# Decode kernel, two passes of attention and feed-forward: new constants in its planner, a new order of loads, two instead of four K units kept

## The chip, the cores and the metric

One core of a Trainium2 chip runs the whole program. The time is device microseconds of one execution; a kernel's figure is the median of its runs, and runs of two kernels are compared only when they were taken in turn on the same chip. "The span" is the profiled execution from its first to its last record, about 1.8 us shorter than the time of that run. PE is the engine that multiplies matrices (PEld its weight loads), DVE the vector engine, ACT the scalar engine, SPq the queue that issues the loads, SBUF the core's memory on the chip.

## The reference, cut to what matters

An attention block with cached K and V and a gated feed-forward block, applied twice, for a batch of four and one token each. Weights and caches are the same in both passes, so every K and V byte is needed twice.

```python
B, Sq, D = 4, 1, 512
Hq, Hkv, Sk, Dh = 32, 8, 8192, 128          # k_cache, v_cache: (B, Hkv, Sk, Dh) bf16
...
x = x + attention(layernorm(x), k_cache, v_cache, wq, wo)
x = x + (silu(xn @ w_gate) * (xn @ w_up)) @ w_down       # xn = layernorm(x)
x = x + attention(layernorm(x), k_cache, v_cache, wq, wo)
x = x + (silu(xn @ w_gate) * (xn @ w_up)) @ w_down
```

K is 64 MiB and so is V; read in both passes this is 256 MiB. SBUF holds all weights and 11 slots of 1 MiB, so nearly everything must stream in twice.

## The kernel before

A **unit** is 1 MiB of K or V: half of one head's cache for one batch. The program is made by a small planner: steps with guessed durations for PE, DVE and ACT, and a list of loads in a fixed order. The planner plays them through, and the order in which it starts them is the order of the instructions in the program. What the chip then does waits only on semaphores. The order of the loads is a string of tokens: `K` the next K unit, `P` the next two K units in one load of 2 MiB, `a`/`b` a V unit of the first or second pass (batch, head, half), `A`/`B` both halves in one load, `c` a second-pass V unit that needs no load because its first-pass copy is **kept** in its slot, `wq wo0 wg1 ...` weight pieces. The code is cut, and its comments are added here.

```python
class Plan:
    HOP = 0.06
    PAGE = 5.0          # us to fetch 256 PE instructions
    PAGE_N = 256
    LOAD_LEAD = 2.1     # us from issue to first data
    LOAD_TAIL = 2.1     # us from last data to landing
    ...
                s.start = t                       # a slot is free, the queue issues
                sp_at = t + 0.35
                dma_at = max(dma_at, t + self.LOAD_LEAD) + s.us
                s.end = dma_at + self.LOAD_TAIL
    ...
ORDER = ("c100 c101 P c260 x P c300 c301 c261 wq P wg1 c120 P c340 P K K c341 P P wo1 A06 P wo0 P a010 K c240 "
    ...
NSLOT = 11
KM = (4, 0, 0, 0)       # K units of batch 0..3 that stay in their slots for the second pass
    ...
        if u not in kept_k:
            st.slot_of = home[u]      # the slot comes free after these matmuls
    ...
        if u[1] == 1 and ("k", 0) + u[2:] in kept_k:
            home[u] = ("k", 0) + u[2:]            # second pass of a kept unit: no load
        else:
            loads[u] = load_pair(u)
```

A kept unit saves one load and holds one of the 11 slots for as long as it waits. In each batch a serial chain lies between the passes: output projection, feed-forward, the next query projection. Until it is done the batch's second-pass K can be loaded but not consumed.

## Time and profile before

| what | before |
|---|---|
| time, median of 4 | 638.88 us (638.27 to 640.04) |
| span of the profiled run | 636.9 us |
| bytes read from memory | 256.12 MB, 402 GB/s over the span |
| PE / DVE busy | 397.1 / 402.7 us |
| load queue busy, as a share of 16 DMA engines | 97.7% |
| landing of the last load, and the end after it | 626.25 us, 10.7 us |

The queue of loads is the bound; PE and DVE have over a third of the span to spare. A list made from the trace is used all through this text: for each load its issue, its landing (the completion semaphore's last update), the distance from the landing before, and how far **ahead** it was issued, meaning the time from its issue to the landing of the load before it. A load that is ahead enough lands one transfer time after the previous one; a load that is not leaves a gap.

### The profile page before, as it was taken

To read this page: it belongs to the slowest core of one execution; us is meant where nothing else is said; L and a number is where in the kernel's file an instruction comes from. 1 tells how busy PE (TensorE), PEld (TensorE's weight loads), DVE (VectorE), ACT (ScalarE), POOL (GpSimd) and SP (SyncE) were. 2 spreads that over 40 slices of the span, in tenths; PEclk is the share of its full clock that TensorE was granted. 3 is DMA by queue.
4 is the path that set the end of the run, shared out by engine and by line. 5 is a ranking of instruction groups with operands and counts; after the bars stand their busy time and mean duration, and the time that the engine had idled before them with its cause. 6 is when DMAs were issued, how large, how long until landed. Compare 5 with 4: busy or idle time off the path is not lost.

```text
span 636.9 us, 18609 instructions
## 1 busy us (share of the span) xinstructions
PE 397.1 (62%) x8689; PEld 205.1 (32%) x8689; DVE 402.7 (63%) x615; ACT 40.4 (6%) x107; POOL 1.8 (0%) x8
## 2 busy tenths in 40 slices
PE   0375444454786675677576665578667676856686
PEld 0221211113542141135421241333431244721265
DVE  4477764365236958876579777366667863489832
ACT  1000200002000020000200100000100020000100
POOL 1000000000000000000000000000000000000000
PEclk9997686657557767667667778555575667568686
DMA  8999999999989999999999999999999999999991
GB/s 356 423 426 412 405 417 423 420 418 401 387 348 400 422 418 419 420 412 421 402 408 419 422 425 428 417 408 420 418 408 421 415 419 421 417 409 419 423 425 65
DMA packets 37237, 257.32 MB, mean 404 GB/s; under 512 B 3492, under 2 KB 9384, under 8 KB 10664
## 3 DMA queue, kind: packets, MB, share of 16 engines
q1 hardware_dynamic: 37160, 256.14, 97.7%
q8 instruction: 68, 1.11, 0.7%
q14 instruction: 9, 0.07, 0.0%
HBM read 256.12 MB, written 0.00 MB: 402 GB/s over the span
## 4 chain that ended last, share of the span: by engine, by line
DMA 63%; PE 18%; DVE 16%; issue 2%; SPq 0%; ACT 0%
DMA pool<-in_A_k_cache_dram 39%; DMA pool<-in_A_v_cache_dram 18%; DVE pool L606 12%; PE ps L622 7%; PE ps L763 5%; DMA wq_sb<-in_A_wq_dram 3%; PE ps L472 2%; DMA wo_sb<-in_A_wo_dram 2%; DMA wq_sb<-in_A_k_cache_dram 2%; DVE wq_sb L606 1%; PE ps L809 1%; PE ps L726 1%; DVE ps L790 1%; PE ps L681 1%; PE ps L873 1%
## 5 line engine op out<-in xcount | busy, mean ns | idle before, releaser
L606 DVE STREAM_TRANSPOSE pool<-pool 128x2048 uint32<-128x2048 uint32 x116 | 264.8, 2300 | 70.8 <-DMA pool<-in_A_k_cache_dram 70.6
L622 PE MATMUL ps<-pool,qpad 32*32 32x512 bf16 x3840 | 190.6, 543 | 127.2 <-DVE pool L606 120.7
L622 PEld LDWEIGHTS ps<-pool,qpad 32*32 32x32 bf16 x3840 | 54.6, 108 | 240.1 <-DVE pool L606 179.6
L763 PE MATMUL ps<-pool,pp 128*32 128x256 bf16 x1936 | 100.0, 366 | 43.1 <-DMA pool<-in_A_v_cache_dram 31.6
L763 PEld LDWEIGHTS ps<-pool,pp 128*32 128x32 bf16 x1936 | 57.5, 122 | 81.6 <-DMA pool<-in_A_v_cache_dram 42.8
L790 DVE STREAM_TRANSPOSE ps<-ps 128x256 f32<-128x256 f32 x62 | 28.4, 458 | 74.7 <-PE ps L763 74.4
L645 ACT ACTIVATE pp<-ps,negm 128x512 bf16<-128x512 f32 x32 | 21.6, 686 | 329.6 <-DVE negm L641 306.5
L726 PE MATMUL ps<-oT,wo_sb 128*128 128x4 bf16 x640 | 23.0, 167 | 12.6 <-DVE oT L794 9.2
L726 PEld LDWEIGHTS ps<-oT,wo_sb 128*128 128x128 bf16 x640 | 20.7, 103 | 24.7 <-DVE oT L794 16.7
L641 DVE TENSOR_REDUCE negm<-ps 128x1 f32<-128x512 f32 x32 | 19.9, 683 | 12.1 <-PE ps L622 12.1
L472 PE MATMUL ps<-xnT,wq_sb 128*128 128x4 bf16 x640 | 18.3, 166 | 12.1 <-DMA wq_sb<-in_A_wq_dram 11.4
L472 PEld LDWEIGHTS ps<-xnT,wq_sb 128*128 128x128 bf16 x640 | 17.7, 104 | 14.5 <-DMA wq_sb<-in_A_wq_dram 11.5
L606 DVE STREAM_TRANSPOSE wq_sb<-wq_sb 128x2048 uint32<-128x2048 uint32 x8 | 18.1, 2290 | 3.5 <-DMA wq_sb<-in_A_k_cache_dram 3.4
L681 PE MATMUL ps<-ident,pp 128*128 128x128 bf16 x128 | 16.0, 311 | 6.3 <-DVE pp L670 5.8
L622 PE MATMUL ps<-wq_sb,qpad 32*32 32x512 bf16 x256 | 13.2, 547 | 8.5 <-DVE wq_sb L606 8.5
L458 ACT ACTIVATE lnv<-var,eps_sb 128x4 f32<-128x4 f32 x10 | 3.0, 298 | 218.0 <-DVE var L453 218.0
L681 PEld LDWEIGHTS ps<-ident,pp 128*128 128x128 bf16 x128 | 12.7, 143 | 12.5 <-DVE pp L670 7.6
L792 DVE TENSOR_REDUCE osum<-ps 128x4 f32<-128x32 f32 x62 | 11.9, 191 | 2.1
L794 DVE TENSOR_TENSOR oT<-osum,invL 128x4 bf16<-128x4 f32 x62 | 10.5, 169 | 2.1
L670 DVE TENSOR_SCALAR pp<-pp,alpha 128x512 bf16<-128x512 bf16 x32 | 9.0, 346 | 1.8 <-ACT alpha L663 1.8
L690 ACT ACTIVATE pp<-ps 128x1024 bf16<-128x1024 bf16 x8 | 8.2, 1024 | 26.9 <-PE ps L681 26.9
L438 PE MATMUL ps<-xx,onesm 128*128 128x32 f32 x20 | 6.3, 410 | 5.3 <-DVE xx L433 4.3
(68 smaller groups left out, 149.4 us busy)
## 6 DMA issues: line engine op xcount, KB each, us to landing
pool<-in_A_k_cache_dram SPq DMA_DIRECT2D x86, 1024.0 KB, 9.7
pool<-in_A_v_cache_dram SPq DMA_DIRECT2D x82, 1024.0 KB, 10.0
pool<-in_A_k_cache_dram SPq DMA_DIRECT2D x15, 2048.0 KB, 15.8
pool<-in_A_v_cache_dram SPq DMA_DIRECT2D x10, 2048.0 KB, 16.6
wq_sb<-in_A_k_cache_dram SPq DMA_DIRECT2D x6, 1024.0 KB, 13.6
wq_sb<-in_A_wq_dram SPq DMA_DIRECT2D x1, 4096.0 KB, 22.0
wo_sb<-in_A_wo_dram SPq DMA_DIRECT2D x4, 1024.0 KB, 16.2
wq_sb<-in_A_k_cache_dram SPq DMA_DIRECT2D x1, 2048.0 KB, 10.3
```

What stands on the lines that cost most here:

```text
L472: op("pe", lambda e: e.matmul(ps[:, bk * BW + h * B:bk * BW + (h + 1) * B], lhsT=wq_sb[:, kt, h * Dh:(h + 1) * Dh], rhs=xnT[:, kt * B:(kt ...
L606: op("dve", lambda e: e.transpose(v, v), reads=keys, writes=keys)
L622: op("pe", lambda e: e.matmul(ps[32 * c:32 * (c + 1), a * BW:(a + 1) * BW], lhsT=qpad[rows, qbuf, es_, g, :], rhs=ap[h][rows, :, es_ // 2, ...
L641: op("dve", lambda e: e.tensor_reduce(negm[:, q, a:a + 1], bank(a), AX.X, ALU.max, negate=True), reads=[f"pb{a}"], writes=[f"negm{q}_{a}"])
L645: op("act", lambda e: e.activation(pblk(q)[:, :, a, :], bank(a).rearrange("p (t j) -> p t j", j=32), ACTF.Exp, bias=negm[:, q, a:a + 1], s ...
L670: op("dve", lambda e: e.tensor_scalar(seg, seg, alpha[:, q, a:a + 1], None, op0=ALU.mult), reads=[f"pp{q}_{a}", f"alpha{q}"], writes=[f"pp ...
L681: op("pe", lambda e: e.matmul(stg[:, t * P:(t + 1) * P], lhsT=pp[:, q, blk * P:(blk + 1) * P], rhs=ident[:], is_transpose=True, start=True ...
L726: op("pe", lambda e: e.matmul(ps[:, OPJ * BW + nq * B:OPJ * BW + (nq + 1) * B], lhsT=wo_sb[:, h, nq * P:(nq + 1) * P], rhs=oT[:, l, h, :], ...
L763: op("pe", lambda e: e.matmul(ps[32 * n:32 * (n + 1), bk * BW:bk * BW + 256], lhsT=pp[:, q, col:col + 32], rhs=v[:, 8 * f:8 * (f + 1), 32 ...
L790: op("dve", lambda e: e.transpose(blk, blk), reads=[f"pb{bk}"], writes=[f"pb{bk}"])
L792: op("dve", lambda e: e.tensor_reduce(osum[:], diag, AX.X, ALU.add), reads=[f"pb{bk}"], writes=["osum"])
L794: op("dve", lambda e: e.tensor_tensor(oT[:, l, g * REP:(g + 1) * REP, b], got, invL[:, q, g * REP:(g + 1) * REP], ALU.mult), reads=[f"pb{b ...
```

## The change

The intent: make the planner's picture of loads and of instruction fetch closer to the chip, and search an order that does well on average when landings come late. The new model charges a load 1.05 us or more when the queue has less than 2.0 us of data left at its issue, and a charge that fades from 1.05 us to nothing where the queue has 2.0 to 3.7 us left. By the planner's own tail of 2.1 us, that is 5.8 us ahead of a landing. The order that came out of the search gives up two kept K units.

```diff
-    PAGE = 5.0
+    PAGE = 5.8
+    PAGE_IDLE = 3.8
-    LOAD_LEAD = 2.1
+    LOAD_LEAD = 2.0
+    LOAD_SOFT = 1.05
+    LOAD_EASE = 3.7
+    def late(self, ahead):
+        if ahead < self.LOAD_LEAD:
+            return max(self.LOAD_LEAD - ahead, self.LOAD_SOFT)
+        return max(0.0, self.LOAD_SOFT * (self.LOAD_EASE - ahead) / (self.LOAD_EASE - self.LOAD_LEAD))
-                dma_at = max(dma_at, t + self.LOAD_LEAD) + s.us
+                dma_at += self.late(dma_at - t) + s.us
+                page = self.PAGE if there < dma_at else self.PAGE_IDLE
-ORDER = ("c100 c101 P c260 x P c300 c301 c261 wq P wg1 c120 P c340 P K K c341 P P wo1 A06 P wo0 ...
+ORDER = ("P P c120 c241 P wd1 c370 x wq c121 wo2 P P K K c371 P P P a021 P a060 a040 c240 P a061 ...
-KM = (4, 0, 0, 0)
+KM = (2, 0, 0, 0)
-            return PL.load(4.914, fn, u0, u1)      # a pair
+            return PL.load(4.924, fn, u0, u1)
-                return PL.load(2.505, fn, u)       # one unit
+                return PL.load(2.51, fn, u)
... (the rest of ORDER is cut)
```

No operation on the chip is added or removed except the two loads and their two transposes (and that 22 instead of 27 loads are pairs).

## The prediction

> **What bounds the kernel now.** I read the page first (time slices, queues, chain), then a table of stretches around the only visible dip, then what the queue that issues the loads waited for there, and last each load in the trace from issue to landing (its completion semaphore).
>
> ```profile
> DMA  8999999999989999999999999999999999999991
> GB/s 356 423 426 412 405 417 423 420 418 401 387 348 400 422 418 419 420 412 421 402 408 419 422 425 428 417 408 420 418 408 421 415 419 421 417 409 419 423 425 65
> ...
> q1 hardware_dynamic: 37160, 256.14, 97.7%
> q8 instruction: 68, 1.11, 0.7%
> ...
> DMA 63%; PE 18%; DVE 16%; issue 2%; SPq 0%; ACT 0%
> ```
>
> The reader is to see that one load queue keeps the 16 DMA engines busy for 97.7% of the span and that the rate is flat at 410 to 428 GB/s in nearly every slice. PE and DVE are busy 62% and 63% and are not the bound; their shares of the chain are short waits between loads. So the end is set by: start, plus bytes over rate, plus stretches in which the queue ran dry, plus the work after the last landing. The slices have one real dip, at about 175 to 191 us, so I cut the stretch finer:
>
> ```profile
> 180.00:184.00 4.00, 3.00 (x125) 2.71 (x123) 0.69 (x3) 0.00 (x0) 0.00 (x0) 0.50 1.00 416
> 184.00:194.00 10.00, 9.02 (x240) 4.39 (x236) 3.36 (x5) 0.00 (x0) 0.00 (x0) 0.66 0.78 274
> 194.00:204.00 10.00, 4.82 (x100) 1.66 (x88) 7.45 (x6) 0.00 (x0) 0.00 (x0) 0.68 1.01 421
> 204.00:610.00 406.00, 273.80 (x5682) 135.25 (x5683) 283.74 (x421) 28.19 (x75) 0.00 (x0) 0.65 1.01 418
> ```
>
> The last two columns are the DMA share and GB/s. From 204 to 610 us the queue is never short (418 GB/s on average, shares at 1.01). From 184 to 194 it is. The waits of the issuing queue and its issues say why:
>
> ```profile
> SPq L92 <- PE ps L622: 12.4, 3, 10.1
> SPq L62 <- PE ps L763: 10.2, 4, 8.8
> ...
> 175.70 0.33 SPq L92 DMA_DIRECT2D pool<-in_A_k_cache_dram  x1
> 176.69 10.76 SPq L92 DMA_DIRECT2D pool<-in_A_v_cache_dram  x2
> 188.13 18.36 SPq L92 DMA_DIRECT2D pool<-in_A_k_cache_dram  x11
> ```
>
> Between about 177 and 187 us no load can be issued: all 11 slots hold a unit (a unit is 1 MiB of K or V), and PE works through the feed-forward and query chain of batch 0 before it can consume second-layer K. The load issued at 187.12 lands 5.75 us after the one before it, where 2.48 us is usual. **That is 3.3 us lost, and it is the only load of 216 that came too late.** For the rest, the distance between landings is 2.48 us for 1 MiB alone and 4.89 us for 2 MiB in one transfer, plus some 12 us spread thinly over the kernel (0.1 us every fifth load, 0.5 to 1.2 us at ten or so places). These fall on loads issued 5 to 13 us ahead too, so an order of loads does not cure them. The last landing is at 626.25; 10.7 us of serial work (output projection, last feed-forward, store) follow.
>
> **What the Trainium skill says.** "Perfetto Trace Analysis", section "Identifying the Most-Contended Engine", wants DMA judged by memory rate, not by busy engines; here both agree. "DMA: Bandwidth & Descriptors", section "Where 436 GB/s comes from", puts the fabric ceiling at 435 GB/s; the flat 418 to 428 is 96 to 98% of it, so no schedule can make the bytes much faster. The same page, section "Measured", gives 1 MB 341 GB/s and 16 MB 425: the trace agrees with the trend only weakly, 1 MiB per 2.48 us being 423 GB/s and 2 MiB per 4.89 us 429, because queued loads overlap. "Runtime: NRT & Kernel Launch", section "Instruction fetch mechanics", has the instructions refilled in 16 KiB blocks of 256 and the cost mostly hidden. The trace agrees on the size (68 packets, 1.11 MB); hidden it is not on PE (weight loads of the score matmuls wait 53.5 us for "issue"), but it hardly shows on the load queue.
>
> **The change part by part.** All of it is the plan: the constants of the scheduler's model, the order of loads, and how many K units of batch 0 stay in SBUF for the second layer (KM from 4 to 2). No operation differs.
>
> 1. *Bytes.* I counted the tokens of both orders. Before: 16 K pairs and 96 single K tokens, 4 of these kept, so 124 K units loaded; 107 V units; 231 MiB. After: 14 pairs and 100 singles, 2 kept, so 126 K; V again 107 (21 kept in both): 233 MiB. Two more units of 2.48 us: **+4.96 us**, on the path, since the queue is the bound.
> 2. *Pairs.* Before 16 K, 7 + 4 V = 27 two-MiB transfers; after 14 + 4 + 4 = 22. A pair saves 2 x 2.48 - 4.89 = 0.07 us; five fewer: **+0.35 us**.
> 3. *Weights.* The same ten pieces and the query weights, earlier or later: 0.
> 4. *DVE and PE.* Two K units more to transpose at 2.30 us each: 4.6 us of DVE, which is 63% busy: hidden. Matmul counts are equal.
> 5. *The stall at the first chain.* The question is whether the new order removes the 3.3 us. I wrote both orders as lists of loads with running sums (2.48, 4.89, and 2.25 to 2.96 us for weight pieces). Before, the last weight that batch 0's chain needs is at 164.0 of this sum; after it, 164.2. Slots held through the chain: before, 4 K + 2 V of batch 0 and 1 V of batch 1; after, 2 K + 4 V. The slots are full at 176.4 before and 176.6 after. The built instruction order of PE is the same there too: down-projection, two V units, query projection, one K unit, two V units, more K. So the two units given back on the K side are taken again on the V side, and **the dry spell should come again**. One gain: the gate weights are there at 159.3 and the output weights at 152.1 (before, 156.5 for the last of these), so the chain may start about 1 us sooner. I take 0.5 us off.
> 6. *The other three chains.* Between the last first-layer V of a batch and the first K of its second layer the sums leave 35, 35 and 17 us of loads in the new order, as in the old, where none of the three ran dry: 0. The beginning has the query weights third pair later (sum 27.2 instead of 19.7), with 11 slots, two weight pieces and the query weights queued, which reach to about 47 us by the landing times, while K is consumed from about 36.5: no dry spell. I allow +0.3 us for something small.
>
> Sum: 638.8 + 4.96 + 0.35 - 0.5 + 0.3 = 643.9. An author picks an order because it does well, and the model's new curves may see a stall that I cannot see by counting, so I lean a little lower: **643.4 us**.
>
> **The rivals.** (a) *The new order removes the dry spell*: 638.8 + 5.3 - 3.3 = 640.8. For it: the order was chosen over delayed landings, and this dip is what such a choice would go for. Against: the slot count above. (b) *The change wins*, below 638: it would need more than 5.3 us back, and the trace has only 3.3 us of late loads and a fixed 10.7 us tail; only if the thin 12 us were due to the order. I see no sign. (c) *PE or a new dry spell becomes the limit*: rotating units through 11 slots with only two kept K to free at once after the chain, or the long runs of K (13 in a row in PE's order), could starve the queue again: 3 to 5 us more, 646 to 649. For it: kept V are held longer than kept K. Against: in such runs before, loads were issued 5 us or more ahead throughout.
>
> **Range and chances.** Low end: rival (a) with run-to-run scatter (the three runs span 638.27 to 640.04), 640.2. High end: the stall stays and another of its size comes, 647.0. Two per cent is 12.8 us: faster needs more than every idle microsecond of the queue, 0.01; slower needs three stalls on top of the bytes, 0.02; within, 0.97.
>
> **What would show each step.** Bytes read from memory should rise from 256.1 to 258.2 MB. Landings should stay 2.48 and 4.89 us apart; if they don't, the rate is not fixed and my sum falls. The last landing should move from 626.25 to about 631, with 10.7 us after it; a changed tail is a step that I left out. The slice at about 185 us should dip again: if it is flat, rival (a) holds and step 5 was wrong; a dip elsewhere is rival (c). If the total falls although the bytes rose, the thin losses were the schedule's after all, and that would make the prediction wrong.

## The result, and the profile after

| what | before | after |
|---|---|---|
| time, median of 4 | 638.88 us | 643.79 us (642.20 to 644.54) |
| ratio, 95% interval | | 1.0071 (1.0047 to 1.0096) |
| span of the profiled run | 636.9 us | 640.4 us (the fastest of its four) |
| last landing, and the end after it | 626.25, 10.7 us | 629.71, 10.7 us |
| PE / DVE busy | 397.1 / 402.7 us | 396.0 / 407.5 us |

The kernel became 0.7% slower, by some 4.9 us; that counts as the same at a threshold of 2%, but it is clear of the noise.

The page of the kernel after, its slices of DMA, its load queue and its memory line:

```profile
DMA  8999999999999999999999999999999999999992
GB/s 362 396 425 419 425 415 412 417 426 389 404 359 423 422 418 421 420 418 421 417 418 422 419 421 424 427 419 397 397 422 421 420 417 422 382 410 421 423 425 86
...
q1 hardware_dynamic: 38168, 258.23, 98.0%
...
HBM read 258.22 MB, written 0.00 MB: 403 GB/s over the span
```

The reader is to see the same picture with 2.1 MB more in it: the same flat rate and the same dip in the twelfth slice (359 now, 348 before). The load queue is no less full than it was, and it has more to carry. The same stretches as those of before in the prediction (the last two columns are the DMA share and GB/s):

```profile
180.00:184.00 4.00, 3.09 (x116) 2.83 (x112) 0.70 (x4) 0.00 (x0) 0.00 (x0) 0.50 1.01 420
184.00:194.00 10.00, 7.32 (x192) 3.44 (x192) 7.60 (x8) 0.00 (x0) 0.00 (x0) 0.79 0.84 325
194.00:204.00 10.00, 5.19 (x120) 1.71 (x128) 8.17 (x5) 0.00 (x0) 0.00 (x0) 0.73 1.01 426
204.00:614.00 410.00, 272.11 (x5712) 131.37 (x5696) 283.26 (x423) 28.18 (x75) 0.00 (x0) 0.65 1.01 417
```

The dry spell at 187 us is still there, milder in this run: 325 GB/s in place of 274. The issuing queue's waits from 170 to 195 us say that it is the same wait, for matmuls that free a slot:

```profile
SPq L62 <- PE ps L772: 11.7, 4, 8.6
SPq L92 <- PE ps L631: 9.7, 2, 9.2
SPq L62 <- PE ps L631: 3.1, 1, 3.1
```

What was bought with the two units is seen in the list of issues: the last column is the median time from issue to landing. First the kernel before, then the kernel after:

```profile
pool<-in_A_k_cache_dram SPq DMA_DIRECT2D x86, 1024.0 KB, 9.7
pool<-in_A_v_cache_dram SPq DMA_DIRECT2D x82, 1024.0 KB, 10.0
```

```profile
pool<-in_A_k_cache_dram SPq DMA_DIRECT2D x92, 1024.0 KB, 11.6
pool<-in_A_v_cache_dram SPq DMA_DIRECT2D x88, 1024.0 KB, 12.0
```

Loads wait about 2 us longer in a deeper queue, and there are more of them. Before, 38 loads of one unit were issued 5.5 to 6 us ahead; after, none was. But those 38 landed 2.48 us (median) after the load before them, as loads issued 10 us and more ahead do (2.49). **The depth was paid for with two loads and bought nothing that the chip had been charging.**

The landings of the two profiled runs, summed up, with 2.48 us a unit, 4.89 a pair and the weights' own times taken as the base:

| term | before to after |
|---|---|
| first landing (9.15, then 8.72) | -0.4 us |
| two more units | +5.0 us |
| five fewer pairs | +0.35 us |
| the late load at 187 us (3.3, then 1.0) | -2.3 us |
| thin losses spread over the kernel (11.7, then 12.6) | +0.9 us |
| last landing (626.25, then 629.71) | +3.5 us |

Most of the thin losses have one shape: a single landing about 1 us late, every 65 to 85 us. In the changed kernel these are seven of 1.0 to 1.24 us, 7.8 of its 12.6 us, all on loads issued 6 to 16.5 us ahead. Their cause is open (see the last section).

### The profile page after: what moved, and what is told of

Same layout as the page of the kernel before. It is cut to its first block, busy times and chain, and to the rows that moved or that the text cites. A ratio compares the mean times of both kernels' runs of the same rounds, so it can differ in the third digit from the quotient of the medians.

```text
span 640.4 us, 18628 instructions
## 1 busy us (share of the span) xinstructions
PE 396.0 (62%) x8689; PEld 202.1 (32%) x8689; DVE 407.5 (64%) x617; ACT 40.4 (6%) x107; POOL 1.8 (0%) x8
## 3 DMA queue, kind: packets, MB, share of 16 engines
HBM read 258.22 MB, written 0.00 MB: 403 GB/s over the span
## 4 chain that ended last, share of the span: by engine, by line
DMA 67%; PE 16%; DVE 13%; SPq 3%; issue 1%
DMA pool<-in_A_k_cache_dram 39%; DMA pool<-in_A_v_cache_dram 19%; DVE pool L615 10%; PE ps L631 7%; PE ps L772 4%; DMA wq_sb<-in_A_k_cache_dram 4%; DMA wq_sb<-in_A_wq_dram 3%; SPq L92 3%; DMA wo_sb<-in_A_wo_dram 2%; PE ps L481 1%; DVE wq_sb L615 1%; PE ps L818 1%; PE ps L882 1%; PE ps L690 1%; PE ps L735 1%
## 5 line engine op out<-in xcount | busy, mean ns | idle before, releaser
L615 DVE STREAM_TRANSPOSE pool<-pool 128x2048 uint32<-128x2048 uint32 x118 | 269.8, 2301 | 64.7 <-DMA pool<-in_A_k_cache_dram 64.2
L772 PEld LDWEIGHTS ps<-pool,pp 128*32 128x32 bf16 x1936 | 55.9, 120 | 88.0 <-DMA pool<-in_A_v_cache_dram 46.9
L481 PEld LDWEIGHTS ps<-xnT,wq_sb 128*128 128x128 bf16 x640 | 17.6, 103 | 11.4 <-DMA wq_sb<-in_A_wq_dram 7.1
L690 PE MATMUL ps<-ident,pp 128*128 128x128 bf16 x128 | 14.3, 283 | 2.4 <-DVE oT L803 1.4
L690 PEld LDWEIGHTS ps<-ident,pp 128*128 128x128 bf16 x128 | 11.2, 131 | 8.8 <-DVE selw L710 4.0
L818 PE MATMUL ps<-xnT,wu_sb 128*128 128x4 bf16 x280 | 8.9, 167 | 0.9 <-DVE hT L874 0.5
```

What stands on the lines that cost most here:

```text
L481: op("pe", lambda e: e.matmul(ps[:, bk * BW + h * B:bk * BW + (h + 1) * B], lhsT=wq_sb[:, kt, h * Dh:(h + 1) * Dh], rhs=xnT[:, kt * B:(kt ...
L615: op("dve", lambda e: e.transpose(v, v), reads=keys, writes=keys)
L690: op("pe", lambda e: e.matmul(stg[:, t * P:(t + 1) * P], lhsT=pp[:, q, blk * P:(blk + 1) * P], rhs=ident[:], is_transpose=True, start=True ...
L772: op("pe", lambda e: e.matmul(ps[32 * n:32 * (n + 1), bk * BW:bk * BW + 256], lhsT=pp[:, q, col:col + 32], rhs=v[:, 8 * f:8 * (f + 1), 32 ...
L818: op("pe", lambda e: e.matmul(ps[:, bk * BW + (fo - f0) * B:bk * BW + (fo - f0 + 1) * B], lhsT=w_sb[:, kt, fo * P:(fo + 1) * P], rhs=xnT[: ...
```

## The experiments

The theory, called **counting** below: the time is the loads, one after the other at a fixed distance, plus what is lost where a load is issued too late, about 4 us or less ahead. (The first expectation still said about 2 us; the limit was moved before the ten-slot runs.) The first rival is **depth**, the changed kernel's own model: loads issued up to 5.8 us ahead lose time, so a deeper queue is worth bytes. The second is that the new constants change the program through the placement of instructions on PE and DVE. All experiments computed the right result.

### Bytes without the new order: two K units kept, old order, old constants

```diff
-KM = (4, 0, 0, 0)
+KM = (2, 0, 0, 0)      # in the kernel before
```

> The old order and the old constants with two instead of four K units of batch 0 kept: two units more to load, no other edit. Counting theory (the time is the loads at 2.48 us a unit, plus the loads issued too late, about 2 us or less before the one ahead has landed): plus 4.96 us, minus the 3.3 us of the dry spell at 187 us if the two freed slots end it, so 640.5 us; 643.8 if the spell stays or a new one comes elsewhere (a late load after 350 us is possible, where two K pairs and two V pairs follow each other). Rival (the order itself, not the bytes, made the change slower): about 638.9, as before.

Measured: 643.19 us (before in these rounds 638.53), ratio 1.0073 (1.0055 to 1.0090). This one line costs what the whole change costs. The two freed slots did end the spell at 187 us, but another came at 370 us: a load issued 1.27 us ahead, 2.7 us lost. Its stretches:

```profile
184.00:194.00 10.00, 5.12 (x144) 2.65 (x144) 6.19 (x6) 0.00 (x0) 0.00 (x0) 0.76 1.01 416
...
368.00:378.00 10.00, 7.22 (x162) 6.27 (x162) 5.01 (x18) 1.12 (x2) 0.00 (x0) 0.75 0.80 307
```

From 184 to 194 the rate is 416 GB/s now, and the share is whole; the hole has moved. So 4.96 less 3.3 plus 2.7 is 4.4, and 4.7 was measured. The rival "the order, not the bytes" falls. The new order with the same two kept units, run in the same rounds (the next experiment), took 643.72: the order by itself adds or saves nothing clear of the noise.

### The constants alone, in both directions

The order and number of kept units of one kernel with the planner constants of the other.

```diff
# e2: the kernel after
-ORDER, KM of after
+ORDER, KM of before
# e3: the kernel before
-ORDER, KM of before
+ORDER, KM of after
```

> Old order and old number of kept units with the new constants of the scheduler's model: the same loads in the same order; only where PE and DVE instructions stand can move. Counting theory: as before, 638.9, within 1 us, the one late load at 187 us included. Rival (the new constants alone change the time through the order on PE): outside 637.5 to 640.5.

> New order and two kept K units with the old constants of the model: what the order and the kept units do without the new constants. Counting theory: as the changed kernel, 643.8 within 1 us, one late load at about 187 us of 1 to 3 us. Rival (the constants made the difference): near 639.

Measured: 638.89 us for the old order under the new constants, ratio to before 1.0003 (0.9986 to 1.0020); 643.72 us for the new order under the old constants, ratio 1.0074 (1.0053 to 1.0095). So the constants act through the order that they choose; whatever else they do is within the noise (0.2%, some 1.3 us). The late load is in both traces: 3.5 us lost at 187 us in the first, 2.6 us in the second (issued 1.36 us ahead, where the profiled run of the changed kernel had 1.94). The stretch of the spell, in the first and in the second:

```profile
184.00:194.00 10.00, 7.96 (x240) 3.90 (x240) 3.36 (x5) 0.00 (x0) 0.00 (x0) 0.83 0.81 302
```

```profile
184.00:194.00 10.00, 7.72 (x198) 3.50 (x192) 6.19 (x8) 0.00 (x0) 0.00 (x0) 0.75 0.78 302
```

Both ran at 302 GB/s there. So the changed kernel's milder spell was probably that run's more than the order's: it was also the fastest of its four, by 1.2 us. That is one trace of each, so it is not shown.

### What a pair is worth

```diff
-"... P c260 x P ... A06 ..."     # in the kernel before, all 27 pairs
+"... K K c260 x K K ... a060 a061 ..."
```

> The kernel before with each of its 27 two-MiB loads split in two loads of 1 MiB at the same place: a pair is worth 2 x 2.48 - 4.89 = 0.07 us by the landings, so counting theory expects 27 x 0.07 = plus 1.9 us, 640.8. Rival (pairs are worth nothing at this queue depth): 638.9. Rival (pairs save an issue and a late load each): over 643.

Measured: 639.88 us, ratio 1.0016 (0.9998 to 1.0035). The 27 pairs together are worth 1.0 to 1.35 us by ratio and by medians, 0.04 to 0.05 us each, a little less than the 0.07 of the landings; the interval's low end, 0.9998, does not exclude no effect at all.

### How far ahead must a load be issued: ten slots

Both kernels were run with one slot less, so that the same loads are issued later.

```diff
-NSLOT = 11
+NSLOT = 10
```

> The changed kernel with 10 instead of 11 slots: the same loads, each issued later, since a slot comes free later. Counting theory (a load costs extra only when it is issued under about 4 us before the landing ahead of it, and then only what is missing): three dry spells before 200 us (loads 18, 44 and 59 issued 0 to 9 us after the one ahead has landed), a few of 1 us later, some 663 us in all. Rival, depth theory (the new constants: any load issued under 5.8 us before the landing ahead loses up to 1 us): about 677 us.

> The kernel before with 10 instead of 11 slots. Here some forty loads will be issued 3 to 4 us before the landing ahead of them, which is what tells the two theories apart: the spacing of their landings is 2.48 us if depth is worth nothing down to there, or up to 3.5 us if it is. Counting theory: about 688 us in all. Rival, depth theory (soft loss below 5.8 us): about 708 us.

Measured, in one execution each, so that their state is unknown: 664.52 us for the changed kernel and 685.68 for the kernel before (before with 11 slots beside them: 637.66). Counting had said 663 and 688, depth 677 and 708 (both from the planner's arithmetic, with the old and the new constants). The changed kernel's trace has its three spells before 210 us, of 1.1, 11.4 and 5.3 us. The second trace holds loads at all distances, so the curve that the change is about can be read from it directly. The distance between landings of 1 MiB loads, by how far ahead they were issued:

| ahead, us | loads | median distance, us |
|---|---|---|
| 3 to 3.5 | 20 | 3.27 |
| 3.5 to 4 | 14 | 3.25 |
| 4 to 4.5 | 11 | 2.83 |
| 4.5 to 5 | 17 | 2.49 |
| 5 to 5.5 | 12 | 2.47 |
| 5.5 to 6 | 14 | 2.47 |
| 10 and more | 35 | 2.48 |

So this run lost about 0.8 us at 3 to 4 us ahead, and nothing in the medians from 4.5 on. On the point that was to tell the theories apart, the expectation for counting (2.48 us at 3 to 4 ahead) was wrong; it did not fit the theory's own limit of about 4 us either, and the 688 came from a planner that charges a load under 4.2 us ahead.

The loss at 3 to 4 us is of this run, and not shown as a rule of the distance alone: its single loads there took from 2.43 to 4.60 us, and the ten loads of 1 MiB that were issued 3 to 4 us ahead in the ten other traces took 2.46 to 3.11 (median 2.5). That nothing is lost from 4.5 us on, by the medians, is in these traces too: 17 loads at 4.5 to 5, 69 at 5 to 5.5 and 200 at 5.5 to 6, each group with a median of 2.48. The new constants let a loss run on to 5.8, and there the kernel before had most of its shallow loads. Two equal stretches in the middle, first of this ten-slot run, then of the kernel before, show the same in the rate:

```profile
380.00:450.00 70.00, 43.68 (x843) 20.17 (x834) 42.18 (x62) 4.10 (x10) 0.00 (x0) 0.60 0.98 394
450.00:520.00 70.00, 46.87 (x950) 24.16 (x942) 40.96 (x75) 5.25 (x15) 0.00 (x0) 0.52 0.97 371
```

```profile
360.00:430.00 70.00, 44.01 (x956) 23.77 (x952) 43.28 (x71) 4.61 (x12) 0.00 (x0) 0.70 1.01 420
430.00:500.00 70.00, 49.41 (x996) 23.52 (x988) 47.93 (x76) 4.75 (x13) 0.00 (x0) 0.56 1.01 416
```

With ten slots the queue really is too short (394 and 371 GB/s); with eleven it is not (420 and 416, as 417 in the long stretch of the changed kernel).

The planner itself, played without a chip, shows how the curve chose. These are its own guesses, no measurements: with the new constants it ends before's order at 640.5 us and the new one at 637.9; with `LOAD_SOFT` set to 0 at 632.1 and 636.5. The chip's spans are 636.9 and 640.4. It is the soft term alone that turned the two orders round in the model; without it the difference is 4.4 us, and the chip's is 3.5 in the spans and 4.9 in the medians.

### One more slot for one more load

```diff
-KM = (2, 0, 0, 0)      # in the kernel after
+KM = (1, 0, 0, 0)
```

> The changed kernel with one K unit of batch 0 kept instead of two: one more unit to load, one more free slot while batch 0's chain runs. Counting theory: plus 2.48 us for the unit, minus the late load at 187 us (1.0 to 2.6 us in the two runs of this order so far), so plus 0 to 1.5 us over the changed kernel: 643.8 to 645.3 us, and no landing gap at 187 us. Rival (the late load does not come from held slots): 646.3 us with the gap still there.

Measured: 644.77 us, ratio to before 1.0108 (1.0093 to 1.0123), so 6.9 us above before's 637.85 in its own rounds. The changed kernel was 4.9 us above before in its rounds. One kept unit less therefore costs 1.0 us by the bare times, which are of different rounds, and 2.0 to 2.4 us by the differences and the ratios; only the first lies in the expected 0 to 1.5. What the trace settles is the spell. Its stretch is full in this kernel:

```profile
184.00:194.00 10.00, 7.98 (x187) 3.41 (x184) 7.50 (x9) 0.00 (x0) 0.00 (x0) 0.67 1.01 411
```

The load that was late is now issued 4.2 us ahead and loses 0.2 us. So held slots do make the spell, and a unit (2.48 us) is a poor price for 1 to 2.6 us of spell.

### A version that should beat both

A search over orders with the soft loss cut to what the ten-slot trace shows gave two candidates.

```diff
-    LOAD_LEAD = 2.0 / LOAD_SOFT = 1.05 / LOAD_EASE = 3.7 / PAGE = 5.8 / PAGE_IDLE = 3.8
+    LOAD_LEAD = 1.9 / LOAD_SOFT = 0.8 / LOAD_EASE = 2.7 / PAGE = 5.2 / PAGE_IDLE = 4.2
-KM = (2, 0, 0, 0)
+KM = (3, 0, 0, 0)      # f1, with a new ORDER of 43 pairs; f2 has (4, 0, 0, 0) and 30 pairs
```

> An order found by search with the scheduler's late-load curve cut to what the ten-slot runs show (no loss from about 4.7 us before the landing ahead): 232 units (three K and 21 V kept), 43 pairs, no late load at batch 0's chain. Counting theory against before: plus 2.48 us for one unit, minus 16 more pairs at 0.05 to 0.07 us = 0.8 to 1.1, minus 3.3 us of dry spell: about 637.0 us, 1.6 us faster than before. Rival, depth theory with the new constants: 640.1 against 640.5 for before, so the same time as before.

> The same search from the old order: 231 units as before (four K and 21 V kept), 30 pairs, one late load at batch 0's chain as before. Counting theory: 638.5 less 3 pairs (0.2 us), and the late load kept at about 2 to 3 us: 637.5 to 638.5. Rival, depth theory: 638.4 against 640.5 for before, 2.1 us faster.

Measured: 638.66 us for both (before in these rounds 637.85), ratios to before 1.0007 (0.9992 to 1.0022) and 1.0009 (0.9996 to 1.0023). Neither beats the kernel before. The second lies 0.2 us over the upper end of what counting expected; its late load lost 2.2 us, and depth's 2.1 us gain is not there. The first missed its expected gain of 1.6 us; taken alone, it is what depth had said (the same time as before), and it is the second that speaks against depth. In the first, the late load at batch 0's chain is gone as planned:

```profile
184.00:194.00 10.00, 8.56 (x248) 4.41 (x252) 5.43 (x6) 0.00 (x0) 0.00 (x0) 0.81 0.91 364
```

The rate is still only 364 GB/s, because one of the landings that come 1 us late falls here (at 191.68 us, issued 13.7 us ahead). Besides, the trace has 1.1 us of two loads issued 2.6 and 4.8 us ahead at 310 us, and its thin losses sum to 14.7 us in a profiled run that was the slowest of its six, against 11.7 before. Why those grew is open; that pairs are worth less than was booked may be part of it. So counting does not explain this kernel in full.

## Why the prediction was right

The time on record was 643.4 us and 643.79 came out, within the range. By its steps:

1. *Bytes, +4.96 us.* Right. It is the step that carries the result. Memory reads rose from 256.12 to 258.22 MB, the landings kept their 2.48 us, and the one-line experiment with two fewer kept units cost 4.7 us by itself, with one spell traded for another.
2. *Pairs, +0.35 us.* Too small to be tested: at the 0.04 to 0.05 us a pair of the experiment five are 0.2 to 0.25, and no effect at all was not excluded.
3. *Weights, 0.* Nothing in the landings contradicts it; not tested alone.
4. *DVE and PE hidden.* Right: DVE is 4.8 us busier and the tail after the last landing is 10.7 us in both.
5. *The spell comes again, half a microsecond milder.* The spell was right: same place, same wait, and it goes when a slot is freed. Its size varies more than a step of 0.5 allows: 2.3 us milder in the changed kernel's profiled run, 0.7 us milder in the twin with old constants. Of the 2.3, 0.5 is the issue (186.58 in place of 187.12 us), 0.6 the later landing ahead of it, and 1.1 a shorter time from issue to landing (5.39 in place of 6.53 us). The reason given for the 0.5 did not hold. By the prediction's own sums the last of gate and output weights comes later (159.3, before 156.5). The feed-forward did begin 0.8 us sooner (166.15, before 166.99), but then PE waited 1.34 us for a V unit and began the query projection 0.3 us later than before. That the load was issued sooner all the same was luck: before, PE waited 0.98 us for "issue" just ahead of the matmuls that free the slot, and after it did not. The twin without that wait issued at 187.15 us, no sooner than before. The lines, first before, then after:

```profile
178.73 1.87 PE L472 MATMUL ps<-xnT,wq_sb 128*128 128x4 bf16 x64
186.01 1.05 PE L622 MATMUL ps<-pool,qpad 32*32 32x512 bf16 x16 [0.98 <-issue]
```

```profile
175.89 1.05 PE L772 MATMUL ps<-pool,pp 128*32 128x256 bf16 x16 [1.34 <-DMA pool<-in_A_v_cache_dram]
179.07 1.87 PE L481 MATMUL ps<-xnT,wq_sb 128*128 128x4 bf16 x64
```

6. *The other chains, 0, and a small allowance.* Right: no other load was late by the changed kernel's trace. What grew were the thin losses, by 0.9 us.

The 0.5 us by which I leaned below my sum (643.9), because an author picks an order that does well, was not borne out: the sum alone was nearer, though 0.5 us is within the scatter of the runs (642.20 to 644.54). In the two profiled runs the last landing moved by only 3.5 us, to 629.71 where about 631 was expected: the spell lost 1.8 us less than booked, the thin losses 0.9 more. So that the medians came within 0.4 us of the forecast is in part luck. One reading of the slices was loose: 28 of the 40, not nearly all, lie at 410 to 428 GB/s, and the two before the dip (401 and 387) hold weight pieces, of which the 1 MiB ones of the output projection land 2.87 to 2.98 us apart. Nor is it shown that instruction fetch is not hidden on PE. The 53.5 us that the prediction sets against the Trainium skill ("Runtime: NRT & Kernel Launch", section "Instruction fetch mechanics", which calls the crossing of a 16 KiB block mostly hidden) are waits of the weight loads for "issue", for nothing that the profile shows; the score matmuls themselves waited only 4.5 us for it. Rival (a), the spell removed, is refuted by the trace; (b), a win, would have needed thin losses that follow the order, and they did not shrink; (c), a new spell, did not come in the changed kernel, though it did in the first experiment.

## What to carry to other kernels

Where one load queue is full, price a schedule in loads first: in this kernel a deeper queue was worth nothing beyond the point where the next load's issue is hidden, and that point (here 4.5 to 5 us ahead of a landing) could be read from one trace with a buffer too few. Before a planner's penalty is allowed to choose an order, look up in a trace whether the chip charges it where the planner thinks: here 38 loads in the penalised range landed on time. Keep a unit in SBUF as long as the dry spell that its slot causes costs less than its load.

## What the Trainium skill lacked or had wrong

- "DMA: Bandwidth & Descriptors", section "Measured": 1 MB at 6.15 us and 341 GB/s is one transfer's own span, for loads issued from another engine. In a full queue 1 MiB lands every 2.48 us (423 GB/s), and 2 MiB in one load saves 0.04 to 0.05 us by the split experiment, which does not exclude that it saves nothing. So the gain beyond 1 MB that the table shows (341 to 425 GB/s) did not appear in the queue: 2 and 4 MiB (4.89 and 9.95 us) come to 429 and 422 GB/s. From issue to landing a 1 MiB load took about 6.5 us when little was queued ahead of it (median of the 20 issued 3 to 3.5 us ahead with ten slots: 6.52).
- No page says how far ahead a load has to be issued to keep the queue full: 4.5 to 5 us before the landing of the one ahead. At 3 to 4 us one run lost about 0.8 us a load; ten such loads in other traces lost from nothing to 0.6.
- No page has it: every 65 to 85 us one landing comes about 1 us late whatever its distance ahead (1.18 to 1.23 us at 218.2, 296.8, 367.8, 445.9, 516.9 and 582.7 us in the kernel with one kept unit; 1.5 to 1.6 us in the new order with old constants). Its cause is open.
